# Attention's copies out of PSUM: VectorE in their own tick instead of ScalarE through a queue

## The chip, the cores and the metric

The kernel runs on one core of a Trainium2 chip. The core has five engines, each working through its own instructions in order: TensorE (PE in the profile, with its weight loads as PEld), VectorE (DVE), ScalarE (ACT), GpSimd (POOL) and SyncE (SP, which here only issues DMAs). They wait for one another through semaphores. The metric is the device time of one execution in microseconds (us). Before the change it is 2259.16 us, the median of three runs (2257.97 to 2259.57).

## The reference

Two layers, one behind the other. The first is an attention through 32 inducing points, over 4 batches of 12480 tokens with 128 channels. The second takes every token through a wide layer (128 to 2048 to 128) with a rational function between its two matrix products.

```python
def mab(q, kv):
    s = scale * (q @ kv.transpose(0, 2, 1))
    s = s - s.max(-1, keepdims=True)
    a = np.exp(s); a /= a.sum(-1, keepdims=True) + 1e-09
    return a @ kv
h = mab(I, x)             # 32 rows per batch, pooled over all tokens
x2 = mab(x, h)            # every token weighs those 32 rows
h = x2 @ w_in             # 49920 tokens, 128 -> 2048
P = a[0] + a[1]*h + a[2]*h**2 + a[3]*h**3
Q = 1.0 + abs(b[0])*abs(h) + abs(b[1])*h**2
out = (P / (Q + 1e-06)) @ w_out
```

## The kernel before

**The main work.** A unit is one batch b, one block n of 480 tokens (26 a batch) and one q of eight pairs of feature blocks; there are 4 x 26 x 8 = 832 of them, and `fast_ticks` (the loop over t) handles one per tick. In its tick a unit has two fp16 products of TensorE into a PSUM tile `hp` of three buffers, an absolute value (VectorE's mask over `hp` for even units, `row<-hp`; ScalarE's `AF.Abs` for odd ones), on VectorE a product `line<-row,all,hp`, later VectorE's or GpSimd's last product (`line<-line,all,row`; `finals`) and four fp32 products of TensorE into `po`. Between them ScalarE runs logarithm and sigmoid over several units at once: a table load, three wide logarithms, a table load, three wide sigmoids, which repeats every ten units. I call these ten units a *ten*; ScalarE's every second table load marks one. In the names, `hp2_5_3` is batch 2, block 5, unit 3.

**The side work.** While the units of one batch run, two generators run the attention's next steps in between. `ahead` prepares the next batch: `pass1` (scores of the inducing points, their exponentials in `e`), `pooled` (it turns the weights `e` with TensorE into `pt`, copies `pt` out of PSUM into `eT`, and sums the tokens with them into `ph`, which VectorE adds into `acc`; seven groups a batch), then the pieces of the stacked weights `st` and `linear`, a run of nine small VectorE instructions (`gl`, `st`). `attend` makes the tokens' weights of the batch in work or the next (`pass3`, `quotients`): scores `pd`, a copy `sT`, turned scores `ps`, largest `amx`, difference `a`, exponential, sum `asm`, quotient on GpSimd, turned back by TensorE into `pa`, and from there the fp16 pair `hl`: `hl[0]` is `pa` rounded, `hl[1]` is what the rounding left (`hl<-pa,hl`). Seven groups a batch again. `spread` then sends `hl` with eight DMAs on SP's queue into `at`, from which the units' first products read.

**What sets the order.** Instructions keep the order in which the code issues them. `side` is called at the end of each tick, after the tick's own instructions. It lets each generator go on if the kind that it asks for has budget left: `yield "v", 0.65` asks for 0.65 us of VectorE; the budget grows by 0.36 a tick and is kept up to 1.45 (`SPARE`). One generator issues only one kind per tick (`kind or need`). `"wait"` lets a tick pass. Both generators share one PSUM buffer, `misc` (`ps_m`, one buffer); `holder` keeps the other generator off it until `free`.

**The queue of ScalarE's copies.** `self.act(do)` puts a copy into `act_q` with the tick's number and yields `"wait"` until it is issued. `run_act`, called in each tick ahead of the wide logarithms and sigmoids, issues the entries of earlier ticks; a copy thus stands on ScalarE two ticks behind the TensorE work it follows, and holds `misc` until then. In the code before the main loop (`direct`), the copy is issued at once. The first batch's weights are pooled there, by `first_batch`, which has copies of its own.

Of the kernel before, what the change touches and what calls it, by code (L numbers as in the profile page):

```python
# [16 lines left out]
AF = mybir.ActivationFunctionType  # L17
ALU = mybir.AluOpType
# [3 lines left out]
TP = 120  # L22
# [3 lines left out]
BT = HB * TP  # L26
# [176 lines left out]
class Kernel:  # L203
# [248 lines left out]
    def pooled(self, b):  # L452

        nc, ap = self.nc, self.ap
        e = self.e[b]
        acc = ap.tile([P, C + 1], F32, tag="acc", name=f"acc{b}")
        xs = self.xs.pop(b)

        def turned(g):
            rows = slice(0, M * min(4, self.NB - 4 * g))  # L460
            for c in range(HB):
                yield "pe", 0.22
                if c == 0:
                    pt = self.misc(f"pt{b}_{g}").rearrange("p (c n) -> p c n", c=HB)
                nc.tensor.transpose(out=pt[0:TP, c, rows], in_=e[rows, g, TP * c:TP * c + TP], identity=self.ident[rows, rows])
            eT = ap.tile([TP, HB, P], F32, tag="eT", name=f"eT{b}_{g}", bufs=2)
            yield from self.act(lambda: nc.scalar.activation(eT[:, :, rows], pt[0:TP, :, rows], AF.Identity, bias=0.0, scale=1.0))
            eTs.append(eT)

        eTs = []  # L470
        while self.e_done.get(b, 0) < self.NG:
            self.flush()
            yield "wait", 0
        for g in range(self.NG):
            nb = min(4, self.NB - 4 * g)
            yield from turned(g)
            eT = eTs.pop(0)
            self.free()
            yield from self.landed("x", b, g)
            for k in range(HB * nb):  # L480
                j, c = divmod(k, HB)
                if c == 0:
                    yield "pe", 0.4
                if k == 0:
                    ph = self.misc(f"ph{b}_{g}")
                nc.tensor.matmul(ph[M * c:M * c + M, 0:C + 1], eT[:, c, M * j:M * j + M], xs[4 * g + j][:, c, :], start=(j == 0), stop=(j == nb - 1))
                if c == HB - 1 and 4 * g + j + 4 < self.NB:
                    xs.append(self.x_rows(b, 4 * g + j + 4))
            yield "v", 0.2
            if g == 0:  # L490
                nc.vector.tensor_copy(out=acc, in_=ph[:, 0:C + 1])
            else:
                nc.vector.tensor_tensor(out=acc, in0=ph[:, 0:C + 1], in1=acc, op=ALU.add)
            self.free()
        yield from self.rows_of(b, acc)
# [340 lines left out]
    def quotients(self, b, r, nb, a):  # L836
        nc, ap = self.nc, self.ap
        rows = slice(0, M * nb)
        sm = ap.tile([TP, HB, 4, 1], F32, tag="asm", name=f"asm{b}_{r}")[:, :, 0:nb]
        engine = nc.vector if self.boot else nc.gpsimd  # L840
        yield "v", 0.7
        nc.vector.tensor_reduce(out=sm[:, :, :, 0], in_=a, axis=mybir.AxisListType.X, op=ALU.add)
        yield "wait", 0
        engine.tensor_scalar(out=sm, in0=sm, scalar1=1.0, scalar2=1e-9, op0=ALU.mult, op1=ALU.add)
        yield "wait", 0
        yield "wait", 0
        yield "v", 0.25
        nc.vector.reciprocal(out=sm, in_=sm)
        yield "wait", 0
        yield "g", 1.2  # L850
        engine.tensor_tensor(out=a, in0=a, in1=sm.broadcast_to(a.shape), op=ALU.mult)
        yield "wait", 0
        yield "wait", 0
        while self.spreads >= 2 or self.tick < self.sent[0] + 2 and not self.boot:
            yield "wait", 0
        for c in range(HB):
            yield "pe", 0.25
            if c == 0:
                pt = self.misc(f"pa{b}_{r}")
            nc.tensor.transpose(out=pt[rows, TP * c:TP * c + TP], in_=a[:, c].rearrange("p j m -> p (j m)"), identity=self.ident[0:TP, 0:TP])  # L860
        unit = A16 if self.fast else 1.0
        hl = ap.tile([P, 2, BT], F16 if self.fast else F32R, tag="hl", name=f"hl{b}_{r}", bufs=2)
        yield from self.act(lambda: nc.scalar.activation(hl[rows, 0], pt[rows, 0:BT], AF.Identity, bias=0.0, scale=unit))
        yield "v", 0.65
        nc.vector.scalar_tensor_tensor(out=hl[rows, 1], in0=pt[rows, 0:BT], scalar=unit, in1=self.plain(hl[rows, 0]), op0=ALU.mult, op1=ALU.subtract)
        self.free()
        self.job(self.spread(b, r, nb, hl))
# [449 lines left out]
```

## Time and profile before

| | |
|---|---|
| median of three runs | 2259.16 us (2257.97 to 2259.57) |
| the profiled execution's own time | 2258.94 us |
| its span, first to last instruction | 2256.7 us |
| mean granted TensorE clock | 0.979 of full speed |
| busy share of the span | PE 94%, DVE 94%, ACT 93%, POOL 64%, PEld 43% |

The span begins with the first batch's pooling (to about 112 us) and ends with the last products of the last units (from about 2218 us); between them lie the 832 ticks, 2.5 us each on average. Nearly all instructions carry line 187, that of the helper that records them, so they are told apart by their operation and the tiles they read and write. Two instructions of one engine can overlap by some hundredths of a microsecond in the profile, so that busy time is somewhat less than their number by their mean. TensorE's ends are modelled: a busy PE isn't PE at its peak.

### The profile page before, as it was taken

The numbers are of one execution on the slowest core, as the hardware profiler recorded it, in microseconds if no ns is written. First come the engines' busy times: TensorE is split into PE (matmuls) and PEld (weight loads), VectorE is DVE, ScalarE is ACT, GpSimd is POOL, SyncE is SP. The second block draws the span as 40 slices with busy tenths as digits, with TensorE's granted clock in tenths as the row PEclk, the third lists the DMA queues.
The fourth block names the chain that finished last, engine by engine and source line by source line (L and its number), as shares of the span: only waits on it lengthen the run. The fifth ranks groups of instructions, "written<-read, shape, count | busy, mean of one in ns | idle before, by whom it ended". The sixth has DMA issues, their size and how long they took to land.

```text
span 2256.7 us, 22927 instructions
## 1 busy us (share of the span) xinstructions
PE 2123.9 (94%) x7728; PEld 970.5 (43%) x7728; DVE 2115.2 (94%) x2117; ACT 2096.7 (93%) x1191; POOL 1436.1 (64%) x1018
## 2 busy tenths in 40 slices
PE   4599999999999999999999999999999999999997
PEld 2234444444444444444444444444444444444443
DVE  7699999999999999999999999999999899999995
ACT  1499999998999999998999999989999999999995
POOL 2256766667666666676666766856676766666661
PEclk8789999999999999999999999999999999999999
DMA  8232010230331112112221230010101000000000
GB/s 320 69 94 85 30 32 16 68 84 31 97 96 47 33 49 70 47 51 88 90 60 35 53 84 23 22 35 31 58 18 57 16 16 31 18 22 18 20 15 15
DMA packets 104578, 120.85 MB, mean 54 GB/s; under 512 B 13314, under 2 KB 101250, under 8 KB 104450
## 3 DMA queue, kind: packets, MB, share of 16 engines
q1 hardware_dynamic: 104450, 119.28, 17.1%
q8 instruction: 63, 1.03, 0.2%
q14 instruction: 65, 0.53, 0.1%
HBM read 80.89 MB, written 25.56 MB: 47 GB/s over the span
## 4 chain that ended last, share of the span: by engine, by line
PE 41%; DVE 23%; ACT 20%; issue 11%; POOL 2%; SPq 1%; DMA 1%; ACTq 0%; DVEq 0%; POOLq 0%
PE po L187 27%; ACT row L187 17%; DVE line L187 13%; PE hp L187 9%; DVE row L187 5%; ACT L187 2%; POOL line L187 2%; DVE oT L187 1%; PE ph L187 1%; PE pd L187 1%; PE pc L187 1%; SPq L187 1%; DVE gl L187 1%; DVE asm L187 0%; POOL row L187 0%
## 5 line engine op out<-in xcount | busy, mean ns | idle before, releaser
L187 PE MATMUL po<-line,w_out 128*128 128x480 f32 x3328 | 1558.3, 574 | 7.8 <-DVE oT L187 4.9
L187 DVE SCALAR_TENSOR_TENSOR line<-row,all,hp 128x960 f32<-128x960 f32 x832 | 998.1, 1204 | 53.6 <-ACT row L187 31.4
L187 PEld LDWEIGHTS po<-line,w_out 128*128 128x128 f32 x3328 | 618.8, 191 | 406.9 <-issue 242.3
L187 ACT ACTIVATE row<-row,all 128x3840 f32<-128x3840 f32 (+1 forms) x249 | 737.7, 2964 | 1.0
L187 ACT ACTIVATE row<-row 128x3840 f32<-128x3840 f32 (+1 forms) x250 | 715.7, 2863 | 6.8 <-DVE line L187 5.5
L187 POOL TENSOR_SCALAR row<-line,all 128x960 f32<-128x960 f32 x204 | 217.5, 1066 | 622.1 <-DVE line L187 488.4
L187 PE MATMUL hp<-at,st 128*128 128x480 f16 x1664 | 478.3, 370 | 47.3 <-DVE line L187 44.0
L187 DVE TENSOR_SCALAR row<-hp 128x960 int32<-128x960 int32 x416 | 476.5, 1145 | 17.8 <-PE hp L187 15.5
L187 ACT ACTIVATE row<-hp,all 128x960 f32<-128x960 f32 x416 | 436.5, 1049 | 52.5 <-PE hp L187 47.6
L187 DVE SCALAR_TENSOR_TENSOR line<-line,all,row 128x1920 f32<-128x1920 f32 x212 | 474.0, 2238 | 6.1 <-ACT row L187 6.0
L187 POOL TENSOR_TENSOR line<-row 128x960 f32<-128x960 f32 x204 | 455.6, 2233 | 29.9 <-issue 9.9
L187 POOL TENSOR_TENSOR line<-line,row 128x960 f32<-128x960 f32 x204 | 455.7, 2234 | 17.0
L187 PEld LDWEIGHTS <-st 128*128 128x128 f16 x1872 | 181.4, 98 | 522.8 <-issue 507.2
L187 PE MATMUL hp<-same,by 96*128 96x480 f16 x832 | 239.4, 369 | 23.7 <-DVE row L187 23.4
L187 POOL TENSOR_SCALAR line<-line,all 128x960 f32<-128x960 f32 x204 | 217.8, 1068 | 0.0
L187 ACT ACT_TABLE_LOAD x167 | 214.3, 1283 | 3.5 <-PEq L1310 0.7
L187 PEld LDWEIGHTS <-by 96*128 96x128 f16 x832 | 82.2, 99 | 212.2 <-issue 191.9
L187 DVE TENSOR_SCALAR oT<-po,all 128x480 f32<-128x480 f32 x104 | 74.0, 711 | 27.2 <-PE po L187 26.2
L187 PE MATMUL po<-at,st 128*128 128x480 f16 x208 | 60.0, 371 | 0.0
L187 ACT ACTIVATE e<-e,nmc 128x960 f32<-128x960 f32 (+3 forms) x16 | 15.4, 982 | 29.5 <-DVE nmc L187 29.5
L187 POOL TENSOR_TENSOR line<-line 128x384 f32<-128x384 f32 (+2 forms) x11 | 12.1, 1099 | 39.9 <-DVE line L187 39.9
L187 PE MATMUL pd<-xTb,HT 128*32 128x480 f32 x208 | 29.9, 611 | 1.0 <-DVE hl L187 0.6
(126 smaller groups left out, 607.7 us busy)
## 6 DMA issues: line engine op xcount, KB each, us to landing
xTb<-x_c SPq DMA_DIRECT2D x104, 240.0 KB, 3.5
out<-oT SPq DMA_DIRECT2D x104, 240.0 KB, 2.0
xTa<-x_c SPq DMA_DIRECT2D x78, 240.0 KB, 3.4
x<-x_t SPq DMA_DIRECT2D x78, 240.0 KB, 3.9
at<-hl SPq DMA_DIRECT2D x416, 30.0 KB, 1.8
row<-x_c SPq DMA_DIRECT2D x8, 768.0 KB, 12.7
row<-x_r SPq DMA_DIRECT2D x8, 768.0 KB, 11.2
line<-w_in SPq DMA_DIRECT2D x4, 480.0 KB, 5.5
```

Source lines behind the costliest of these rows:

```text
L187: ins = call(*args, **kw)
```

## The change

Two copies go from ScalarE to VectorE. In `pooled`, the copy of the turned weights, `eT<-pt`, is issued as VectorE's `tensor_copy`; in `quotients`, the rounding `hl[0]<-pa` becomes VectorE's `tensor_scalar` (a product with `unit`). Both ask for 0.65 of VectorE's budget in place of the queue. `act`, `act_q` and `run_act` stay, and nothing puts a copy into the queue any more. `first_batch` keeps its copies on ScalarE.

```diff
@@ pooled.turned
             eT = ap.tile([TP, HB, P], F32, tag="eT", name=f"eT{b}_{g}", bufs=2)
-            yield from self.act(lambda: nc.scalar.activation(eT[:, :, rows], pt[0:TP, :, rows], AF.Identity, bias=0.0, scale=1.0))
+            yield "v", 0.65
+            nc.vector.tensor_copy(out=eT[:, :, rows], in_=pt[0:TP, :, rows])
             eTs.append(eT)
@@ quotients
         hl = ap.tile([P, 2, BT], F16 if self.fast else F32R, tag="hl", name=f"hl{b}_{r}", bufs=2)
-        yield from self.act(lambda: nc.scalar.activation(hl[rows, 0], pt[rows, 0:BT], AF.Identity, bias=0.0, scale=unit))
+        yield "v", 0.65
+        nc.vector.tensor_scalar(out=hl[rows, 0], in0=pt[rows, 0:BT], scalar1=unit, scalar2=None, op0=ALU.mult)
         yield "v", 0.65
         nc.vector.scalar_tensor_tensor(out=hl[rows, 1], in0=pt[rows, 0:BT], scalar=unit, in1=self.plain(hl[rows, 0]), op0=ALU.mult, op1=ALU.subtract)
```

The first place is VectorE in batch 3's pooling, from the first sum `acc3` (`ph3_0` holds it in PSUM). Before, it stands at units 3 and 4 of block 5 of batch 2:

```order
L187 SCALAR_TENSOR_TENSOR line_64<-row_65,all_76,hp2_5_3_7432 128x960
L187 COPY acc3_6869<-ph3_0_7455 128x129
L187 SCALAR_TENSOR_TENSOR line_64<-row_65,all_76,hp2_5_4_7442 128x960
L187 TENSOR_SCALAR row_65<-hp2_5_6_7495 128x960
L187 SCALAR_TENSOR_TENSOR line_64<-row_65,all_76,hp2_5_5_7485 128x960
L187 SCALAR_TENSOR_TENSOR line_64<-line_64,all_76,row_65 128x1920
L187 SCALAR_TENSOR_TENSOR line_64<-row_65,all_76,hp2_5_6_7495 128x960
```

After, the first copy and the first sum stand around units 4 to 7 of block 2:

```order
L187 SCALAR_TENSOR_TENSOR line_64<-row_65,all_76,hp2_2_4_7151 128x960
L187 COPY eT3_0_7178<-pt3_0_7173 120x512
L187 TENSOR_SCALAR row_65<-hp2_2_6_7180 128x960
L187 SCALAR_TENSOR_TENSOR line_64<-row_65,all_76,hp2_2_5_7165 128x960
L187 SCALAR_TENSOR_TENSOR line_64<-line_64,all_76,row_65 128x1920
L187 SCALAR_TENSOR_TENSOR line_64<-row_65,all_76,hp2_2_6_7180 128x960
L187 COPY acc3_6641<-ph3_0_7198 128x129
L187 TENSOR_SCALAR row_65<-hp2_3_0_7228 128x960
L187 SCALAR_TENSOR_TENSOR line_64<-row_65,all_76,hp2_2_7_7190 128x960
```

The copy is new on VectorE, two units ahead of its sum, and batch 3's pooling begins some 20 units earlier. Counted in units of the whole order, batch 3's seven sums stand at units 460 to 508 before and 439 to 469 after; batch 2's at 280 to 332 before and 278 to 320 after; batch 1's at 127 to 161 before and 126 to 158 after.

The second place is VectorE at batch 3's first `hl`, in block 20 of batch 2. Before:

```order
L187 SCALAR_TENSOR_TENSOR line_64<-row_65,all_76,hp2_20_2_9175 128x960
L187 TENSOR_SCALAR row_65<-hp2_20_4_9201 128x960
L187 SCALAR_TENSOR_TENSOR line_64<-row_65,all_76,hp2_20_3_9186 128x960
L187 SCALAR_TENSOR_TENSOR line_64<-row_65,all_76,hp2_20_4_9201 128x960
L187 SCALAR_TENSOR_TENSOR hl3_0_9199<-pa3_0_9194,hl3_0_9199 128x480
L187 TENSOR_SCALAR row_65<-hp2_20_6_9224 128x960
```

After:

```order
L187 SCALAR_TENSOR_TENSOR line_64<-row_65,all_76,hp2_20_2_9175 128x960
L187 TENSOR_SCALAR hl3_0_9199<-pa3_0_9194 128x480
L187 SCALAR_TENSOR_TENSOR hl3_0_9199<-pa3_0_9194,hl3_0_9199 128x480
L187 TENSOR_SCALAR row_65<-hp2_20_4_9201 128x960
L187 SCALAR_TENSOR_TENSOR line_64<-row_65,all_76,hp2_20_3_9186 128x960
L187 SCALAR_TENSOR_TENSOR line_64<-row_65,all_76,hp2_20_4_9201 128x960
```

Rounding and remainder now stand back to back in one tick, two units earlier than the remainder stood. Of the 27 pairs of the main loop 18 stand so; 9 are split over two or three ticks. ScalarE's order loses the copies; the attention's exponentials move with the rest of the side work, and the table loads stay as many.

## Rows read from the trace of the kernel before

**Rows 1.** The page's busy us, share of the span, instructions.

```profile
PE 2123.9 (94%) x7728; PEld 970.5 (43%) x7728; DVE 2115.2 (94%) x2117; ACT 2096.7 (93%) x1191; POOL 1436.1 (64%) x1018
```

**Rows 2.** The chain that ended last, shares of the span by engine.

```profile
PE 41%; DVE 23%; ACT 20%; issue 11%; POOL 2%; SPq 1%; DMA 1%; ACTq 0%; DVEq 0%; POOLq 0%
```

**Rows 3.** Timeline of ACT, a ten with hl, then one without: start, us, instruction.

```profile
2020.53 1.28 ACT L187 ACT_TABLE_LOAD   x1
...
2032.28 0.55 ACT L187 ACTIVATE hl<-pa 64x480 f16<-64x480 f32 x1
...
2045.40 1.28 ACT L187 ACT_TABLE_LOAD   x1
...
2069.83 1.28 ACT L187 ACT_TABLE_LOAD   x1
```

**Rows 4.** Timeline of ACT in batch 1's pooling, one ten with two eT.

```profile
446.87 1.28 ACT L187 ACT_TABLE_LOAD   x1
...
454.30 0.58 ACT L187 ACTIVATE eT<-pt 120x512 f32<-120x512 f32 x1
...
465.75 0.59 ACT L187 ACTIVATE eT<-pt 120x512 f32<-120x512 f32 x1
...
472.29 1.28 ACT L187 ACT_TABLE_LOAD   x1
```

**Rows 5.** Windows of the main loop: stretch and length, then busy us by engine, PEclk.

```profile
112.00:392.00 280.00, 268.87 (x889) 118.55 (x889) 275.10 (x263) 273.44 (x154) 179.55 (x121) 0.97 0.17 52
392.00:504.00 112.00, 111.47 (x560) 54.54 (x558) 103.30 (x94) 111.30 (x68) 74.03 (x68) 1.00 0.28 69
504.00:672.00 168.00, 162.73 (x562) 72.50 (x561) 162.97 (x165) 156.16 (x85) 114.29 (x75) 0.99 0.26 81
672.00:952.00 280.00, 272.65 (x1098) 127.73 (x1096) 264.33 (x247) 277.48 (x162) 186.03 (x146) 1.00 0.17 48
952.00:1064.00 112.00, 106.56 (x360) 48.41 (x360) 107.89 (x112) 103.24 (x58) 78.50 (x55) 0.98 0.20 62
1064.00:1400.00 336.00, 331.34 (x1303) 152.53 (x1302) 321.94 (x297) 331.64 (x190) 221.80 (x166) 1.00 0.21 61
1400.00:1512.00 112.00, 103.16 (x321) 46.91 (x320) 107.74 (x107) 99.73 (x55) 79.52 (x53) 0.95 0.08 26
1512.00:2218.00 706.00, 678.08 (x2161) 308.50 (x2159) 674.16 (x575) 697.43 (x382) 472.93 (x296) 1.00 0.08 26
```

**Rows 6.** Lines by form, the two copies on ACT and like work on DVE.

```profile
L187 ACT ACTIVATE hl<-pa 128x480 f16<-128x480 f32 x24 | 13.4, 558 | 3.1 <-PE pa L187 3.1
L187 ACT ACTIVATE eT<-pt 120x512 f32<-120x512 f32 x18 | 10.5, 585 | 0.0
L187 DVE COPY sT<-pd 128x480 f32<-128x480 f32 x24 | 15.6, 649 | 2.1 <-PE pd L187 2.1
L187 DVE TENSOR_REDUCE amx<-ps 120x16 f32<-120x512 f32 x24 | 16.4, 682 | 1.2 <-PE ps L187 1.2
L187 DVE SCALAR_TENSOR_TENSOR hl<-pa,hl 128x480 f16<-128x480 f32 x24 | 15.6, 650 | 3.9 <-ACT hl L187 3.9
```

**Rows 7.** Timeline of DVE, neighbours with no wait between them.

```profile
1601.49 0.68 DVE L187 TENSOR_REDUCE amx<-ps 120x16 f32<-120x512 f32 x1
1602.10 1.15 DVE L187 TENSOR_SCALAR row<-hp 128x960 int32<-128x960 int32 x1
```

**Rows 8.** Windows, five tens without side work.

```profile
2045.40:2167.53 122.13, 117.05 (x364) 53.35 (x363) 114.77 (x94) 121.84 (x66) 81.25 (x50) 1.00 0.06 19
```

**Rows 9.** Waits: engine line <- releaser: us in total, times, longest us.

```profile
ACT row L187 <- PE hp L187: 47.6, 34, 8.6
PE hp L187 <- DVE line L187: 44.0, 52, 4.9
```

**Rows 10.** Windows, 13 us at batch 3's linear run.

```profile
1459.00:1472.00 13.00, 4.99 (x14) 2.18 (x13) 12.75 (x15) 9.46 (x5) 8.99 (x6) 0.75 0.01 3
```

**Rows 11.** Timeline of SP, the eight DMAs of one at.

```profile
1621.77 4.96 SPq L187 DMA_DIRECT2D at<-hl  x8
```

## The prediction

> **What bounds the kernel now.** I read the page's busy times first: PE, DVE and ACT are each busy for 93 to 94% of the span [rows 1], and the chain of waits is shared among them, 41, 23 and 20% [rows 2]. No engine is the bound for the whole run, so the question is which of them leads in each stretch. For that I read ACT's timeline by tens. A ten without side work lasts from the table load at 2045.40 to that at 2069.83, 24.43 us, and ACT is busy all through it: in five such tens it worked 121.84 of 122.13 us, VectorE 114.77 [rows 3, 8]. A ten with one `hl` copy lasts 24.87 [rows 3], one with two `eT` copies 25.42 [rows 4]. So where ACT leads, a copy lengthens the ten by what it takes on ACT: 0.44 us for an `hl`, (25.42 - 24.43) / 2 = 0.49 for an `eT`.
>
> Then I read the stages of the main loop [rows 5]. In 392 to 504, 672 to 952 and 1064 to 1400, where the three poolings lie, ACT is the fuller engine: 111.30 + 277.48 + 331.64 = 720.4 of 728 us against VectorE's 103.30 + 264.33 + 321.94 = 689.6. So it is in the last stage, 697.43 of 706 against 674.16, where only the last batch's attention is left. In the other four (112 to 392, 504 to 672, 952 to 1064, 1400 to 1512: 672 us), where the stacked weights are made, VectorE is the fuller one, 275.10 + 162.97 + 107.89 + 107.74 = 653.7 us against 632.6.
>
> **What goes and what comes.** In the main loop 21 `eT` and 27 `hl` copies move; the 28th `hl` lies ahead of it, beside an equally long step, and I give it nothing. I price the 3 + 4 smaller ones like the others.
> Off ACT: 27 x 0.44 + 21 x 0.49 = 11.9 + 10.3 = 22.2 us.
> Onto VectorE: no row shows it making these copies. The nearest are `sT`, a copy of 128x480 out of PSUM, 0.649 us, and `amx`, which reads 120x512 from there, 0.682 [rows 6]. A neighbour starts before the one ahead of it is told to end: `amx` at 1601.49 ends at 1602.17, the next starts at 1602.10 [rows 7]. With 0.07 off, an `hl` costs 0.58 and an `eT` 0.61: 27 x 0.58 + 21 x 0.61 = 15.7 + 12.8 = 28.5 us.
>
> The Trainium skill, page "VectorE: DVE Perf Modes", section "The DRAIN you can't avoid", says that the next VectorE operation can't issue until the pipe behind the last one has emptied. By that a copy would cost its whole duration, 27 x 0.65 + 21 x 0.68 = 31.8 us, 3.3 more. The start at 1602.10 [rows 7] lies ahead of the recorded end, so the trace does not agree to the letter, and I stay with the rows.
>
> Over the whole loop the bounds are therefore 22.2 us of gain (ACT leads everywhere) and 28.5 us of loss (VectorE leads everywhere). What of this is on the path is decided stage by stage. I spread the `hl` evenly, one in 78 us (27 over the 2106 us of the loop, seven a batch); the 21 `eT` lie in the poolings.
>
> 1. *Poolings, 728 us.* ACT falls to 720.4 - 9.3 x 0.44 - 10.3 = 706.0; VectorE rises to 689.6 + 9.3 x 0.58 + 12.8 = 707.8. The two are then even, and the fuller engine's work falls from 720.4 to 707.8: -12.6 us.
> 2. *Weight stages, 672 us.* VectorE leads and gets 8.6 x 0.58: +5.0 us.
> 3. *Last stage, 706 us.* ACT leads and loses 9.1 x 0.44: -4.0 us. VectorE, 674.2 + 5.3, stays below ACT's 693.4.
> 4. *Two full engines.* Where ACT alone leads, it idles for little: 728 - 720.4 = 7.6 us in the poolings, 1.0%. Where both are nearly equally full they keep each other waiting: in 112 to 392 (275.10 against 273.44) the fuller one idles for 4.9 of 280 us, 1.75%. The poolings come to be such stages: 1.75% of 707.8 is 12.4 us, +4.8 over what is idle now. The bounds: 0, if they stay as smooth as now, and +19.3, if they come to the 3.8% of 1400 to 1512 (4.3 of 112), where VectorE leads clearly. I take the 1.75%, since that stage is nearest in the two loads.
> 5. *Denser poolings.* In the new order batch 3's seven sums stand within 30 units in place of 48, batch 2's within 42 in place of 52, batch 1's nearly as before. The copy needs two ticks less, so pooling runs faster, and loads VectorE more in less time. A bare ten is 114.77 / 5 = 22.95 us on VectorE [rows 8]. In the 32 units from batch 3's first copy to its last sum, 3.2 tens, come 73.4 + 4.3 (seven `eT`) + 1.5 (seven `acc` of 129 columns, an estimate from `sT`: 0.58 x 129 / 480 = 0.16, with something for the start 0.21 each) + 2.7 (what the tokens' weights need there by the order: two `asm`, two reciprocals, one `hl` pair, an estimate from rows of like size) = 81.9 us, 25.6 a ten. ACT's bare 3.2 tens are 78.2. VectorE thus leads by 3.7 there, and what it has free in the units after can't be used, since ACT's tens are then the limit: +3.7 for batch 3, half of that for batch 2, together +5.6. Below, 0 (neighbouring tens even it out).
> 6. *Waits.* The remainder's wait for ACT's copy goes, 3.9 us in all [rows 6]. In its place VectorE waits for the turned tile from TensorE in its own tick, with the next unit's mask and product queued behind, for which TensorE's next products wait. The like of it is there: 28 `sT` waited 2.1 us for `pd`, 28 `amx` 1.2 for `ps` [rows 6], 0.06 each, so 48 x 0.06 = 2.9. Both are VectorE's, and I put the sum at 0, between -3.9 and +2.9.
>
> Sum: -12.6 + 5.0 - 4.0 + 4.8 + 5.6 + 0 = -1.2 us. Against the profiled execution's own 2258.94 us (2256.7 of span and 2.2 around it) that is 2257.7; this execution lies 0.2 below the median of 2259.16, so I forecast **2258 us**, no change that can be measured. (About 0.2%, 4.5 us, is what a measurement of this kernel can tell from no change.) What the change frees on one full engine it puts on another, somewhat dearer there, and only where that other one had room.
>
> SP's queue: `hl` comes later in the order for some groups (batch 0's fourth stands at unit 89, before at 75, and is needed from 96 on). Eight DMAs take 4.96 us to issue [rows 11], and 6 units last 6 x 2.44 = 14.7. They stay hidden; without this cover TensorE would wait for the difference.
>
> **Rivals.**
>
> *A: the relief of ACT counts in full.* For it: the five bare tens and those with copies follow ACT to the hundredth [rows 3, 4], and VectorE's backlog is worked off over several units. Then terms 4 and 5 are 0 and term 6 is between -3.9 and 0: -11.6 to -15.5, about 2245 us; half of it, with one of the two terms, gives about 2252. Against it: PE is busy for 111.47 + 272.65 + 331.34 = 715.5 of 728 us in the poolings [rows 5]; if those modelled ends are real, the poolings can't fall under it, and term 1 is at most -4.9. Also to this side counts batch 3's `linear`, which follows its VectorE pieces at once before: PE was busy for 4.99 of 13 us there, and its clock fell to 0.75, between the two levels of 1.2 and 2.4 GHz [rows 10]. Now 20 units lie between the pieces and `linear`. The 8.0 us without PE can become shorter by up to some 4.
>
> *B, slower: VectorE takes over from 112 to 1512.* Its sum there is 275.10 + 103.30 + 162.97 + 264.33 + 107.89 + 321.94 + 107.74 = 1343.3 us, ACT's 1353.0. With 18 `hl` and 21 `eT` it has 1343.3 + 10.4 + 12.8 = 1366.5. If the stages can't lend each other time and VectorE idles as much as the fuller engine does now, that is +13.5, less the 4.0 of the last stage: +9.5, 2268.5 us. It decides from the point where VectorE's backlog reaches TensorE: `hp` has three buffers, and TensorE's first products already waited 52 times for VectorE's `line`, 44.0 us, and ACT 47.6 us for TensorE [rows 9]; 18 of the pairs now add 1.16 us at one place in place of 0.58. With term 4's upper bound it goes to about 2278. Against it: in the poolings VectorE has 728 - 689.6 = 38.4 us free for 18.2.
> The Trainium skill, page "Perfetto Trace Analysis", section "Optimizing Scalar/DVE Operations", speaks for B: for an operation that either engine can do it holds offloading to ScalarE sensible if VectorE is saturated, and this change goes the other way. With VectorE and ACT at 94 and 93% [rows 1] the trace gives it no clear case.
>
> *C: the change doesn't do what it says,* since a copy waits for its 0.65 of VectorE's budget as long as for the queue, and the weights come late. In the order the pairs of batch 3 stand two units earlier, batch 0's fourth 14 later. If one group of weights came late by the 5 us of its DMAs, the time would be 2263, or more with a second. The cover above speaks against it.
>
> **Chances and range.** No change (within 4.5 us of 2259.2) 0.40, which is my sum with terms 4 and 5 off by up to a half. A 0.31, all of it faster by over 0.2% (2254.6 and less). B 0.27 and C, with more than one late group, 0.02: slower by over 0.2%. The likeliest case itself goes from 2254 to 2264. The range of 8 in 10 takes in A with its term 6 (2245) and B with most of its upper bound (2274).
>
> **What would show it.** Right: ACT's copies are gone and the bare ten is still 24.43 us; VectorE's two copies take 0.64 to 0.69 us; in the poolings both engines are about equally busy, some 97%; VectorE's share of the chain rises and ACT's falls; the last stage is 3 to 5 us shorter, the weight stages are longer by about as much, and batch 3's pooling shows tens of over 25 us with VectorE full. Wrong: a pooling that is 3 us or more shorter than before per batch with ACT still the fuller one (A); waits of TensorE for VectorE's `line` well over their 44.0 us (B); copies over 0.75 us, or waits of VectorE for `pa` and `pt` of over 3 us, since then my price for VectorE is too low.

## The result, and the profile after

The kernel after takes 2269.86 us (median of 4 runs, 2266.23 to 2275.1) beside 2258.56 us for the kernel before on the same chip (2257.39 to 2259.57). The ratio is 1.0052, 95% interval 1.0035 to 1.0070: slower by some 11 us. It lies in the range that was given, but the forecast, no change at 2258 us, was wrong.

The profiled execution of after took 2266.23 us, the shortest of the four; what follows places the 7 us by which it is longer than the profiled one of before, not all of the 11. Its page's busy times and the shares of the chain answer to [rows 1, 2]:

```profile
PE 2127.3 (94%) x7728; PEld 968.7 (43%) x7728; DVE 2140.8 (95%) x2166; ACT 2078.9 (92%) x1142; POOL 1442.6 (64%) x1018
```

```profile
PE 43%; DVE 27%; ACT 15%; issue 10%; POOL 2%; DMA 1%; SPq 1%; DVEq 0%; ACTq 0%; POOLq 0%
```

The 49 copies (all but those of `first_batch`) have left ACT for DVE, where busy time rises by 25.6 us; ACT's falls by 17.8. ACT's share of the chain falls from 20 to 15%, VectorE's rises from 23 to 27%. By line and form, in us busy and mean ns:

```profile
L187 DVE TENSOR_SCALAR hl<-pa 128x480 f16<-128x480 f32 x24 | 15.6, 652 | 2.6 <-PE pa L187 1.7 <-issue 0.4 <-DMA at<-hl 0.3
L187 DVE COPY eT<-pt 120x512 f32<-120x512 f32 x18 | 12.3, 684 | 0.0
```

652 and 684 ns are `sT`'s 649 and `amx`'s 682 of [rows 6], and the waits are 2.6 us in all. A ten with an `hl` pair, which before lasted 24.87 us [rows 3], is now as short as a bare one, 2040.89 - 2016.46 = 24.43 (ACT's timeline: start, us, instruction):

```profile
2016.46 1.28 ACT L187 ACT_TABLE_LOAD   x1
...
2040.89 1.28 ACT L187 ACT_TABLE_LOAD   x1
```

So the copies cost what the prediction had for them, and the time is not as it had it. The windows of the main loop (stretch, length, then busy us of PE, PEld, DVE, ACT, POOL; then PEclk) beside [rows 5]:

```profile
112.00:392.00 280.00, 267.53 (x895) 118.17 (x894) 274.92 (x264) 273.17 (x150) 182.72 (x120) 0.98 0.17 52
392.00:504.00 112.00, 110.50 (x558) 54.37 (x557) 107.66 (x107) 107.81 (x60) 72.84 (x69) 1.00 0.28 69
504.00:672.00 168.00, 158.55 (x550) 70.22 (x549) 162.46 (x163) 150.16 (x82) 112.92 (x75) 0.98 0.24 76
672.00:952.00 280.00, 273.89 (x1096) 127.52 (x1097) 271.31 (x260) 272.83 (x149) 190.19 (x145) 1.00 0.18 51
952.00:1064.00 112.00, 103.33 (x353) 44.91 (x352) 105.57 (x110) 97.06 (x53) 71.40 (x50) 0.98 0.28 87
1064.00:1400.00 336.00, 328.60 (x1282) 151.66 (x1279) 323.07 (x309) 319.54 (x173) 227.34 (x172) 1.00 0.18 52
1400.00:1512.00 112.00, 106.59 (x333) 48.37 (x332) 109.55 (x104) 108.19 (x60) 75.87 (x51) 0.98 0.05 16
1512.00:2218.00 706.00, 682.51 (x2178) 310.02 (x2177) 680.67 (x585) 698.30 (x376) 479.28 (x299) 1.00 0.09 28
```

Look for a stretch in which *every* engine does less than before, since there the time was lost. There are two: 504 to 672 (PE -4.2, DVE -0.5, ACT -6.0 us) and 952 to 1064 (-3.2, -2.3, -6.2). They are the stretches of batch 1's and batch 2's weight pieces and `linear`. 1400 to 1512, batch 3's, has gained.

To place it by units rather than by time, I set ACT's table loads that begin the same ten beside each other. Units 157 to 187, then 277 to 337 (in after batch 2's pieces lie at its end, in before they follow it), before:

```profile
498.04 1.28 ACT L187 ACT_TABLE_LOAD   x1
...
581.43 1.28 ACT L187 ACT_TABLE_LOAD   x1
...
813.97 1.28 ACT L187 ACT_TABLE_LOAD   x1
...
966.74 1.28 ACT L187 ACT_TABLE_LOAD   x1
```

and after:

```profile
496.62 1.28 ACT L187 ACT_TABLE_LOAD   x1
...
584.95 1.28 ACT L187 ACT_TABLE_LOAD   x1
...
816.43 1.28 ACT L187 ACT_TABLE_LOAD   x1
...
978.14 1.28 ACT L187 ACT_TABLE_LOAD   x1
```

83.39 has become 88.33 us, and 152.77 has become 161.71. The same sum over the whole main loop, after less before, in us (each from one profiled execution):

| units | 7-117 | 117-157 | 157-187 | 187-277 | 277-367 | 367-437 | 437-537 | 537-827 | sum |
|---|---|---|---|---|---|---|---|---|---|
| side work of `ahead` there | (batch 0) | pooling 1 | pieces 1, `linear` 1 | pass 1 of batch 2 | pooling, pieces, `linear` 2 | pass 1 of batch 3 | pooling, pieces, `linear` 3 | none | |
| after | -1.8 | +0.1 | **+4.9** | -1.1 | **+8.6** | +3.9 | -4.4 | -2.7 | +7.7 |

Pooling 1, where nothing else lies, is even (it is hardly denser than before), and the last stage is 2.7 us shorter. Most of the loss is where pieces and `linear` of batches 1 and 2 are; batch 3's stretch has gained. Here is VectorE, GpSimd and TensorE at batch 1's `linear` in after (start, us, engine, instruction, wait and releaser):

```profile
543.31 2.49 DVE L187 SCALAR_TENSOR_TENSOR line<-line,all,row 128x1920 f32<-128x1920 f32 x1
...
543.87 2.40 POOL L187 TENSOR_SCALAR st<-gs 128x512 f16<-128x512 f32 x1
...
547.15 5.99 DVE L187 SCALAR_TENSOR_TENSOR gl<-gl 128x128 bf16<-128x128 f32 x4
...
547.41 2.22 POOL L187 TENSOR_TENSOR line<-row 128x960 f32<-128x960 f32 x1
549.61 1.10 POOL L187 TENSOR_SCALAR line<-line,all 128x960 f32<-128x960 f32 x1
550.79 2.21 POOL L187 TENSOR_TENSOR line<-line,row 128x960 f32<-128x960 f32 x1
553.07 1.74 DVE L187 SCALAR_TENSOR_TENSOR st<-gl 64x128 bf16<-64x128 f32 x3
...
556.21 0.96 PE L187 MATMUL hp<-same,by 96*128 96x480 f16 x2 [7.87 <-DVE row L187]
```

and VectorE at the same run before, with TensorE's wait behind it:

```profile
554.02 2.39 DVE L187 SCALAR_TENSOR_TENSOR gl<-gl 128x128 bf16<-128x128 f32 x4
556.33 0.88 DVE L187 SCALAR_TENSOR_TENSOR st<-gl 64x128 bf16<-64x128 f32 x3
...
560.78 0.73 PE L187 MATMUL hp<-at,st 128*128 128x480 f16 x2 [4.94 <-DVE line L187]
```

The same four instructions take 2.39 us before and 5.99 after, and TensorE stands still for 7.87 us, the mask being queued behind them, where before it stood still for 4.94. (Its granted clock falls behind the wait in both, 0.58 in 560.78 to 564.80 before and 0.54 in 556.20 to 560.20 after, mostly the lower of its levels, 1.2 GHz, so that isn't what differs.) What differs is the place. In after the run falls one unit behind a group of *finals* (VectorE's `line<-line,all,row`, which lets GpSimd begin its four instructions of 1.1 to 2.2 us, once in four units). In before it falls four units behind them, when GpSimd has done with them and has only splits of a weight piece left: it is busy for 1.5 us of the run, against 7.0 after. Narrow windows of VectorE's timeline show one and the same instruction of the four in after, beside GpSimd's at 547.41, and in before, with GpSimd idle:

```profile
547.50 2.28 DVE L187 SCALAR_TENSOR_TENSOR gl<-gl 128x128 f32<-128x128 f32 x1
...
556.12 0.29 DVE L187 SCALAR_TENSOR_TENSOR gl<-gl 128x128 f32<-128x128 f32 x1
```

In after it ends 0.15 us behind GpSimd's. The Trainium skill, page "SBUF — State Buffer", section "SBUF: two separate sides", has the rule: GpSimd and VectorE share one pair of ports to SBUF, and an instruction of VectorE with two inputs there, and one of GpSimd that reads there, take it in turns, each for its whole length. By the code `linear`'s instructions, but for the first and the memset, have two inputs in SBUF; the copies out of PSUM have none. The trace agrees both ways: GpSimd's `st<-gs` at 543.87, elsewhere 0.62 us, took 2.40 beside VectorE's `line<-line,all,row`.

Batch 2's loss has another form. Its four pieces follow each other every second unit, and VectorE waits for a buffer `gs` (there are two) until GpSimd has made the split of the piece but one before, which stands behind the finals in GpSimd's queue. VectorE's timeline in after, with the waits in brackets:

```profile
954.59 0.94 DVE L187 TENSOR_SCALAR gs<-pg,all 128x256 f32<-128x256 f32 x2 [2.90 <-POOL st L187]
...
968.04 0.29 DVE L187 SCALAR_TENSOR_TENSOR gl<-prep,base 128x128 f32<-128x128 f32 x1 [2.28 <-POOL st L187]
```

### The profile page after: what moved, and what is told of

The parts are those of the page before. It is cut to its first block, busy times and chain, and to the rows that moved or that the text cites. A ratio compares the mean times of both kernels' runs of the same rounds, so it can differ in the third digit from the quotient of the medians.

```text
span 2264.2 us, 22857 instructions
## 1 busy us (share of the span) xinstructions
PE 2127.3 (94%) x7728; PEld 968.7 (43%) x7728; DVE 2140.8 (95%) x2166; ACT 2078.9 (92%) x1142; POOL 1442.6 (64%) x1018
## 4 chain that ended last, share of the span: by engine, by line
PE 43%; DVE 27%; ACT 15%; issue 10%; POOL 2%; DMA 1%; SPq 1%; DVEq 0%; ACTq 0%; POOLq 0%
PE po L187 28%; DVE line L187 15%; ACT row L187 13%; PE hp L187 10%; DVE row L187 7%; ACT L187 2%; DVE oT L187 1%; POOL line L187 1%; PE ph L187 1%; PE pc L187 1%; PE pd L187 1%; SPq L187 1%; DVE hl L187 1%; DVE gl L187 1%; PE pg L187 1%
## 5 line engine op out<-in xcount | busy, mean ns | idle before, releaser
L187 PE MATMUL hp<-at,st 128*128 128x480 f16 x1664 | 477.1, 369 | 39.3 <-DVE line L187 36.1
L187 PE MATMUL hp<-same,by 96*128 96x480 f16 x832 | 239.7, 369 | 32.9 <-DVE row L187 32.5
L187 POOL TENSOR_TENSOR a<-a,asm 120x512 f32<-120x512 f32 (+1 forms) x27 | 32.7, 1210 | 0.0
```

The lines of the kernel that those rows point to most:

```text
L187: ins = call(*args, **kw)
```

## The experiments

Each was timed beside the kernel before on the same chip, but not all on one chip, so runs are compared by their ratios to it. The first four set two theories against each other: L, VectorE's load costs; P, the planner's new order does.

**1. The copies on VectorE, through the old queue.** The order of all engines' work is that of before.

```
-  yield from self.act(lambda: nc.scalar.activation(eT..., pt..., AF.Identity, ...))
+  yield from self.act(lambda: nc.vector.tensor_copy(out=eT..., in_=pt...))
```
(`hl` likewise, with tensor_scalar.)

> Both copies run on VectorE, but are issued from the queue, at the place where ScalarE's copies stood; the planner's choices are those of the kernel before (batch 3's seven sums at units 460 to 508, linear at 182, 358, 531). Theory L (the load: 28.5 us more on VectorE is what costs): slower by about as much as the change, +8 to +12 us, 2267 to 2271. Theory P (the packing: the budgeted copies make the side work denser, and that costs): no loss, -6 to +3 us, 2253 to 2262, with ACT's tens 0.44 to 0.49 us shorter per copy in the poolings and the last stage.

2259.87 us, ratio 1.0007 (0.9998 to 1.0016). With the order kept, the engine that makes the copies costs nothing that can be measured. By stages the profiled execution differs from before by +0.1, +1.3 and +0.9 us in units 117-157, 277-337 and 437-487 and by -1.6 in the last stage: no gain in the poolings either. The three runs of `linear`, without their first instruction, take 3.4, 3.4 and 7.9 us, as before.

Why the poolings gain nothing can be read from the ten of [rows 4]. It has no copy on ScalarE any more, and still lasts 471.28 - 445.66 = 25.62 us, 25.42 before. ScalarE's table loads, then the window of the first pooling:

```profile
445.66 1.28 ACT L187 ACT_TABLE_LOAD   x1
...
471.28 1.28 ACT L187 ACT_TABLE_LOAD   x1
```

```profile
392.00:504.00 112.00, 111.57 (x559) 54.54 (x558) 107.39 (x102) 107.64 (x59) 74.24 (x68) 1.00 0.27 69
```

Beside [rows 5], ScalarE falls from 111.30 to 107.64 us, VectorE rises from 103.30 to 107.39, and TensorE stays full, 111.57 of 112 us; in 396 to 498 it waited for others 0.3 us in all. What ScalarE was relieved of it now waits for TensorE: its waits for `hp` rise from 47.6 us [rows 9] to 64.7. In the last stage, where ScalarE leads, the relief shows: of the eight tens that had an `hl` copy before, six fall from 24.9 to 24.4 us.

**2. The new order, copies on ScalarE.**

```
-            nc.vector.tensor_copy(out=eT[:, :, rows], in_=pt[0:TP, :, rows])
+            nc.scalar.activation(eT[:, :, rows], pt[0:TP, :, rows], AF.Identity, bias=0.0, scale=1.0)
```

> Both copies stay on ScalarE, but ask for 0.65 of VectorE's budget and are issued in their own tick, so that the order of everything else is that of the changed kernel (sums of batch 3 at units 439 to 469, linear at 179, 337, 501). Theory L: no slower than before, -3 to +3 us, 2256 to 2262. Theory P: as slow as the changed kernel or nearly, +6 to +14 us, 2265 to 2273, with tens of over 26 us at units 167 to 187, 277 to 337 and 437 to 487.

2322.12 us, ratio 1.028 (1.0265 to 1.0294): far more than the whole change costs, so this run doesn't tell the two apart. Put in its own tick, ScalarE's copy stands behind ScalarE's wide steps, and VectorE's remainder waits for it (waits: us in total, times, longest):

```profile
DVE hl L187 <- ACT hl L187: 62.2, 18, 5.5
```

Before, that was 3.9 us [rows 6]. It shows what the queue is for: a copy on ScalarE has to be issued at the head of a tick, one on VectorE needs no such place.

**3 and 4. One of the two copies alone in its own tick on VectorE,** the other on ScalarE through the queue.

> Only the copies of the turned weights go to VectorE in their own tick; hl's rounding stays in ScalarE's queue. Sums of batch 3 at units 446 to 477, linear at 175, 351, 509. Theory L: 12.8 of the 28.5 us, so a bit under half of the loss, +4 to +6 us, 2263 to 2265. Theory P: it packs the poolings as tightly as the whole change does, so most of the loss, +6 to +12 us, 2265 to 2271.

> Only hl's rounding goes to VectorE in its own tick; the turned weights stay in ScalarE's queue. Sums of batch 3 at units 447 to 481, linear at 183, 348, 511. Theory L: 15.7 of the 28.5 us, a bit over half of the loss, +5 to +7 us, 2264 to 2266. Theory P: the poolings are less dense than after the change, -2 to +5 us, 2257 to 2264.

`eT` alone: 2272.76 us, ratio 1.0055 (1.0042 to 1.0069). `hl` alone: 2271.93, ratio 1.0055 (1.0042 to 1.0069). Either half costs as much as the whole, and both times lie above what L and P allowed for them. Each gives the planner a new order of its own, and in the first two, in the second all three of the runs of nine are long. Batch 1's in the first, batch 3's in the second:

```profile
539.40 6.01 DVE L187 SCALAR_TENSOR_TENSOR gl<-gl 128x128 bf16<-128x128 f32 x4
```

```profile
1426.62 6.95 DVE L187 SCALAR_TENSOR_TENSOR gl<-gl 128x128 bf16<-128x128 f32 x4
```

By VectorE's order, a run that starts one unit behind the finals takes 7.0 to 7.9 us without its first instruction in all kernels so far, and one that starts three or four behind them 3.3 to 4.1; the one exception is `hl` alone in batch 2, three behind, 5.7 us, with GpSimd busy for 4.8 of them. Hence theory G: the place beside GpSimd decides. Its rival D: the poolings are denser, and the long run is only where the lag shows.

**5. After, with `linear` held away from the finals.** By the order only batch 1's run moves, from one to four units behind them.

```
+        while b and self.tick % 4 < 2:
+            yield "wait", 0
         yield "v", 0.6
         self.thirds(b, g)
```

> The kernel after, with the run of nine small VectorE instructions (linear) of batches 1 to 3 held back, where it would fall right behind a new group of GpSimd's finals, until three units have passed. By the order only batch 1's run is moved (one unit behind the finals before, four now). Theory G (the place beside GpSimd's finals costs): that run falls from 8.13 us to about 3.7, TensorE's wait of 7.87 behind it goes, and the time falls by 4 to 6 us, to 2264 to 2266; batches 2 and 3 keep their losses. Rival D (denser poolings cost, the run only shows a lag that comes anyway): the lag turns up elsewhere, the time stays within 1.5 us of 2269.9.

2264.97 us, ratio 1.0024 (1.0013 to 1.0035), beside 1.0052 (1.0035 to 1.0070) of after. The run is short again, and the wait of 7.87 us is gone:

```profile
554.30 2.50 DVE L187 SCALAR_TENSOR_TENSOR gl<-gl 128x128 bf16<-128x128 f32 x4
...
556.72 0.88 DVE L187 SCALAR_TENSOR_TENSOR st<-gl 64x128 bf16<-64x128 f32 x3
```

Units 157-187 go from +4.9 to -0.3 us against before; 277-367 keeps its +8.6. That is G's size and place, though the two intervals touch. (The two profiled executions don't show the gain in their whole: 497-507, where the order is the same, took 4 us more in this one.) Those 4 us begin with the same effect at another place. VectorE's tiny `all<-all,over`, with two inputs in SBUF, fell between two of GpSimd's instructions in after, and into one of them in this execution:

```profile
1414.59 0.15 DVE L187 SCALAR_TENSOR_TENSOR all<-all,over 32x1 f32<-32x1 f32 x1
```

```profile
1411.26 2.15 DVE L187 SCALAR_TENSOR_TENSOR all<-all,over 32x1 f32<-32x1 f32 x1
```

TensorE waited 0.44 us for it in after and 2.45 here, and its granted clock behind that was 1.00 there (1415 to 1418) and 0.57 here (1414 to 1418). So the order alone doesn't settle such a meeting. It may be why after's times (2266 to 2275) and this run's (2259 to 2270) spread more than those of before; that isn't shown.

**6. Before, with `linear` 1 and 2 held until one unit behind the finals.** No copy is moved.

```
+        if b and self.tick % 4:
+            yield "wait", 0
+            while self.tick % 4 != 3:
+                yield "wait", 0
         yield "v", 0.6
```

> The kernel before, copies on ScalarE through the queue, with the run of nine small instructions of batches 1 and 2 held until it falls one unit behind the finals, where batch 3's is already. Theory G: both runs grow from 3.67 us to about 8.2, TensorE waits some 7 to 8 us behind each, and the time grows by 4 to 6 us a batch, to 2267 to 2271: the loss of the change without any of the change. Rival D: nothing of the poolings is denser, so the time stays at 2259 to 2261. The hold of five ticks moves batch 2's pieces too (by 6 units), which by either is worth 2 us at most.

2267.04 us, ratio 1.0038 (1.0025 to 1.0052): most of the loss of the change, without any of the change. Batch 1's part is clean, +4.6 us in 157-187 with its pooling unmoved. For batch 2 the hold moved the pooling too, its sums from units 280-332 to 305-343, so it is denser than in before. Both runs are long (7.7 and 7.6 us), with TensorE waiting 7.25 and 7.05 us behind them. Batch 1's:

```profile
565.96 5.85 DVE L187 SCALAR_TENSOR_TENSOR gl<-gl 128x128 bf16<-128x128 f32 x4
...
571.73 1.73 DVE L187 SCALAR_TENSOR_TENSOR st<-gl 64x128 bf16<-64x128 f32 x3
574.95 0.96 PE L187 MATMUL hp<-same,by 96*128 96x480 f16 x2 [7.25 <-DVE row L187]
```

**7 and 9. Batch 3's run held away from the finals,** in the kernel of run 1 and in the kernel before (the edit of run 5).

> The copies on VectorE but through the queue (order of the kernel before), and batch 3's run of nine held from one to four units behind the finals. Theory G: the run of 8.24 us falls to about 3.7 and TensorE's 7.98 us behind it go: 2252 to 2255. Rival D: 2258 to 2260, for there is nothing denser here to mend.

> The kernel before, copies still on ScalarE, with batch 3's run of nine (linear) held from one to four units behind GpSimd's finals. Theory G: the place alone decides, whoever makes the copies, so the same 2 us off as in the kernel with the queue on VectorE (2256.1): 2255 to 2258. Rival (that gain needed ScalarE's relief): 2258 to 2260.

2256.14 us, ratio 0.9991 (0.9982 to 0.9999), for the first and 2256.75, ratio 0.999 (0.9981 to 0.9999), for the second. In the first the run falls from 7.93 us to 3.23, and TensorE's wait of 7.98 behind it becomes 1.47:

```profile
1471.39 2.27 DVE L187 SCALAR_TENSOR_TENSOR gl<-gl 128x128 bf16<-128x128 f32 x4
1473.58 0.88 DVE L187 SCALAR_TENSOR_TENSOR st<-gl 64x128 bf16<-64x128 f32 x3
1474.88 0.23 PE L187 MATMUL bound<-w_max,mag 128*32 128x4 f32 x2 [1.47 <-DVE mag L187]
```

The gain is the same whoever makes the copies, and at 2 us it is under half of the 4 to 7 that I expected for run 7 (in 437-537 itself, -3.4 and -2.7). Both are a little faster than before; they are the fastest kernels here.

**8. After, the hold of run 5, and every piece held to one in four ticks.**

```
         c = slice(512 * j, 512 * j + 512)
+        while not self.direct and self.tick % 4 != 0:
+            yield "wait", 0
         yield "pe", 0.85
```

> The kernel after with the hold of the run of nine, and the four weight pieces of a batch held to one in four ticks, so that VectorE no longer waits for the buffer gs, which GpSimd's split frees behind its finals (2.90 and 2.28 us in batch 2 of after). Poolings keep their pace of after. Theory G with the buffers as its second half: both losses go, 2256 to 2262. Rival D: the poolings are as dense as in after, so 2266 or more.

2262.56 us, ratio 1.0018 (1.0009 to 1.0027). VectorE no longer waits for `gs` anywhere, and 277-367 falls from +8.6 to +1.9. But pooling 2 starts 26 units later, and other places lose instead: 187-277 +6.2, 537-827 +5.0. Part of that is work that has moved there: batch 3's run now starts at unit 549. The time is just above what G allowed, and well below D.

**10. The kernel of run 1 with each copy made twice.** It tells whether VectorE's copies were free there or paid for by ScalarE's relief.

```
-  self.act(lambda: nc.vector.tensor_copy(...))
+  self.act(lambda: [nc.vector.tensor_copy(...) for _ in range(2)])
```

> The copies on VectorE through the queue (order of the kernel before), each made twice, so 48 more of some 0.65 us, 33 us of VectorE. It tells whether the load cost nothing or was paid for by ScalarE's relief. Theory Z (VectorE's copies lie in time that it has): 2259 to 2262. Rival S (terms 1 to 4 of the prediction were right in size and cancelled, +10 of load against -17 of relief): the second copies bring the load's +5 to +10 and no relief, 2264 to 2270.

2280.5 us, ratio 1.0094 (1.0079 to 1.0110). Copies by line and form:

```profile
L187 DVE TENSOR_SCALAR hl<-pa 128x480 f16<-128x480 f32 x48 | 31.3, 652 | 2.0 <-PE pa L187 1.2
L187 DVE COPY eT<-pt 120x512 f32<-120x512 f32 x36 | 24.7, 686 | 0.6
```

With the smaller ones, 15.6 + 12.3 + 2.6 + 1.3 = 31.8 us of VectorE are added, and the time grows by 2280.5 - 2259.9 = 20.6 (19.7 by the two ratios). This load is far from free. Both theories missed its size: S had put it at 10. The window of the first pooling:

```profile
392.00:504.00 112.00, 110.18 (x553) 53.55 (x552) 109.65 (x106) 106.32 (x58) 72.91 (x68) 1.00 0.25 64
```

VectorE was idle for 8.7 of these 112 us in before, 4.6 in run 1 and 2.4 here, and here TensorE loses 1.4 us. So the first 31.8 us met room on VectorE that the second no longer find. How much of run 1's zero is that room, and how much ScalarE's relief, stays open; the relief shows in the last stage, not in the poolings.

**11. The kernel of run 1, the run of nine cut in three parts, each in a tick of its own.**

```
         V.scalar_tensor_tensor(out=y, ...)
+        yield 'wait', 0
+        yield 'v', 0.4
         cast(mid, y)
```
(once more ahead of the three `st` casts, and a hold ahead of the first part.)

> The copies on VectorE through the queue, and the run of nine (linear) of batches 1 to 3 cut in three, each part in a tick of its own. Theory G: no stretch of VectorE is longer than some 2 us, TensorE's waits of 4.9 us behind the runs of batches 1 and 2 and of 8 us behind batch 3's go, and the time falls to 2248 to 2255. Rival: the parts meet the finals one by one and the pieces are moved later by up to 12 units, so nothing is won over 2256.

2267.78 us, ratio 1.0043 (1.0029 to 1.0056): a miss. TensorE's long waits are gone, but parts still meet the finals, and two instructions then take what four did:

```profile
569.55 2.46 DVE L187 SCALAR_TENSOR_TENSOR gl<-gl 128x128 bf16<-128x128 f32 x2
569.66 2.21 POOL L187 TENSOR_TENSOR line<-row 128x960 f32<-128x960 f32 x1
```

The hold moved the pieces and poolings too, so how much of it is the parts stays open.

**12. After, the hold of run 5, and the pieces of batch 2 alone held to one in four ticks.**

```
+        while b == 2 and self.tick % 4 != 0:
+            yield "wait", 0
         yield "pe", 0.85
```

> The kernel after with the hold of the run of nine (as in the run that moved batch 1's), and the pieces of batch 2 alone held to one in four ticks. In the profiled runs the loss of after was +4.9 us in units 157 to 187, +8.9 in 277 to 337, and less than nothing in all other units together. Theory G, second half (the pieces two ticks apart make VectorE wait for GpSimd's splits, 2.9 and 2.3 us, and that loss stays): 277 to 367 falls from +8.6 to some +2, and the time from 2265 to 2258 to 2261, no longer slower than before by more than 1 per mille. Rival (batch 2 loses because pooling 2 is denser): the waits of VectorE for the splits go, and the time stays at 2264 to 2266.

2257.57 us, ratio 0.9994 (0.9985 to 1.0003), against 1.0024 (1.0013 to 1.0035) of run 5. The loss is gone, with all copies on VectorE in their own ticks and the poolings as dense as in after. The waits for `gs` at the pieces are gone, and TensorE's waits for VectorE's `row`, 32.5 us in after and 23.4 in before, come to 21.8 (us in total, times, longest):

```profile
PE hp L187 <- DVE row L187: 21.8, 24, 4.2
```

By stages, against before, in us:

| units | 7-117 | 117-157 | 157-187 | 187-277 | 277-367 | 367-437 | 437-537 | 537-827 | sum |
|---|---|---|---|---|---|---|---|---|---|
| run 5 | +0.5 | +0.1 | -0.3 | -0.9 | +8.6 | +3.9 | -0.8 | -1.8 | +9.4 |
| run 12 | -1.7 | +0.1 | -0.3 | -0.9 | +4.5 | +3.6 | -3.3 | -0.6 | +1.5 |

Not all of it is as I expected: of the 8.6 us in 277-367 4.1 went in place of some 6.6, and 437-537, where the hold moves batch 3's pieces from units 475-481 to 480-505 and its `linear` from 501 to 507, gave another 2.5. (The 2.2 of units 7-117 are one execution against another; the order there is the same.) Both are places of pieces and `linear`, which agrees with G; how the waits for `gs` and the rest share batch 2's loss, and why 367-437 keeps some 4 us in after and in runs 5, 8 and 12, isn't settled.

## Why the prediction was wrong

The step that made the 11 us is a term that was not there, the place of later work; term 1 failed as well, and its error was covered by chance. The sum priced the copies by load (terms 1 to 4), their density (5) and their waits (6), and took the rest of the order as given. The new ticks also moved every later piece and `linear` against the finals, and there lie +4.9 us, by the run beside GpSimd's finals, and +8.6, for which the pieces' waits account in part. [Rows 10] had such a place: PE busy for 4.99 of 13 us at batch 3's `linear`. I read it as a matter of batch 3, counted it in rival A as a gain of up to 4, and did not ask why batch 1's and 2's runs, by the same line, take 3.4 us, nor where the order puts them now. Batch 3's gain did come (-4.4 in 437-537), and more than that was lost at the other two.

- *Durations*: right. 652 and 684 ns, ScalarE's ten 24.43, waits 2.6 us (term 6).
- *Term 1 with 4, poolings -7.8*: the path was wrong. The term took the fuller of ScalarE and VectorE for what bounds the poolings and left TensorE out, whose 715.5 of 728 us stand in the prediction only against rival A (there, with -4.9 as the most that could come). Run 1, where nothing else changes, shows +2.3 us over the three poolings, with TensorE busy for 111.57 of 112 us in the first. So 0.49 us for an `eT` [rows 4] was no price: that ten is as long without the copies. Another 31.8 us on VectorE cost 20.6 (run 10; the second copies meet a fuller engine than the first, so this is rather the upper price), where terms 2 and 4 had 9.8.
- *Term 2, weight stages +5.0*: not seen apart from the losses in 157-187 and 277-367; run 1 has +0.8 and -0.3 in 157-277.
- *Term 3, last stage -4.0*: -2.7 in after, -1.6 in run 1. Right in sign, too big.
- *Term 5, denser poolings +5.6*: not seen as such. Run 12 keeps the density without the loss. Its +4.5 in 277-367, pieces and `linear` included, is about the most that can be in it for batch 2.
- *Rival B* (2268.5) came nearest to the time, by another way than it said: it wanted TensorE's waits for `line` well over 44.0 us, and they are 36.1; what grew are the waits for `row`, 23.4 to 32.5, of which 7.87 is the one behind `linear`. (Its upper end, 2278, doesn't follow from its terms: 2268.5 with term 4's 19.3 is 2288.) *C* did not come: no unit waited for late weights.

Without the losses in 157-187 and 277-367 the forecast's number would have stood: run 12 and run 1 are both within 0.1% of before. That is partly luck. Without term 5, which run 1 doesn't have, the sum is -6.8 us, and run 1 measured +1.6 (-0.5 to +3.6 by its interval); term 5's +5.6, not seen, hid most of the error of the other terms.

## What to carry to other kernels

When a change moves work in a planner's order, look through the order for everything behind it that has a good and a bad place, above all small VectorE instructions with two operands in SBUF beside GpSimd's, and price each by its place in the new order. Then test the order by itself: the same instructions on the new engine in the old order, and the old instructions moved to the new place, told load and place apart here. That either half cost as much as the whole was a sign that the order was at work. And before relief of one engine is counted as time, look at the busy time of every engine in that stretch: here ScalarE's went into waits for TensorE.

## What was not expected of the hardware

Eight small VectorE instructions on SBUF (seven of 128 columns, a memset) took 2.2 us with GpSimd idle (batch 0's run, at 92.48 in before), 3.4 with it busy for 1.5 of them and 7.9 with it busy for 7.0; the units' instructions with one operand in PSUM kept their 1.2 us beside it. A single VectorE instruction of 32x1 took 0.15 or 2.15 us by whether it met GpSimd's. And the first 31.8 us more on a VectorE that is busy for 94% of the span cost nothing that could be measured (with the copies off ScalarE), the second 31.8 us 20.6.
